# The written-out order of all five queues, shifted by small steps, in an attention and two-MLP kernel on one core

## The chip, the core and the metric

The kernel runs on one NeuronCore of a Trainium2 chip. The core has five engines with a queue each, and each executes its queue in order: TensorE (PE, matmuls, with the weight loads PEld beside it), VectorE (DVE), ScalarE (ACT), GpSimd (POOL) and SyncE (SP), which here issues the DMAs. The metric is the device time of one execution in microseconds, the median of several runs.

## What is computed

The input of 4 x 768 tokens goes through three parts: a gated delta-rule attention (8 heads of 48), an MLP whose token mixing is the real part of a two-dimensional Fourier transform, and an MLP whose token mixing is by two matrices.

```python
for t in range(S):                                   # attention, per batch and head
    y[t] = q[t] @ state
    state = state + b[t] * outer(kn[t], v[t] - kn[t] @ state)
x = y                                                # 4 x 768 x 384
u = x + real(fft(fft(x, axis=1), axis=2))            # first MLP
ch = relu(layernorm(u) @ w_ch1) @ w_ch2              # 384 -> 1536 -> 384
x = u + ch
theta = x @ w_theta                                  # second MLP
yr, yi = w_tok_r @ (x * cos(theta)), w_tok_i @ (x * sin(theta))
u = x + yr + yi
return u + relu(u @ w_ch)
```

## The kernel before

The attention is done by chunks of 64 tokens. `gram` multiplies keys and queries of a chunk (tiles `sm`, PE L351) and ACT evacuates them into `KQ` (L384); POOL moves a part of them within `KQ` (L386). `solve` inverts a triangular block on DVE: a transpose of `KQ` into `T` (L397), then thirty pairs of steps, `tmp` (L434) and `T` (L437), and a scaling (L438). Chunk pairs are numbered 0 to 23, and four of them make one solve, so that there are six solves, 0 to 5. `solved` transposes the result twice, into `TN` (L446) and `TT` (L448). `chunks` then makes for each chunk `pa` from `TN`, `A` (ACT L518), `pt` from `TT`, parts of `YU` by copies (L485) and by ACT (L531), and `pw`, which ACT evacuates into `YU` (L537). `scan` carries the state from chunk to chunk: `pu` (evacuated into `X`, L555 and L556), `ps` (into `X`, L566 and L567) and `py` (into `y`, L581 and L583). After the early phase `sm`, `pa`, `pt` and `pw` take turns in one PSUM bank (pool `psw`, `NMW` = 1).

While this runs, the weights of the first MLP, which are given as 64-bit floats, are converted chunk by chunk (`Split.steps`): DMA L239, ACT L242, four or five DVE steps (L243 to L249) and three PE matmuls into a tile whose name ends in `s` (L251 to L253). A chunk is named by its weight, its row block and its column, for instance `w1_2_768`.

When the first batch is scanned, `fourier_inputs` adds and subtracts six tiles `y` on DVE (L610), with two scalings on ACT (`y4` L626, `y1` L631), and folds them (L610). `fourier_1` multiplies the folds by cosines and sines (`pg`, PE L671). Then come `ffn_up` (`ph` L204 to L206, ACT `hh` L802, DVE `hl` L803) and `ffn_down` (`pc` L812 to L815, DVE `u` L818, store `x2scr` L819), twelve blocks of tokens, with the later scans in between.

The token mixer loads `xt` from `x2scr` (SP L1056), transposes it (`tt`, PE L1059), computes theta (`pth`), reduces it to a remainder `r` (DVE L1073 to L1075), takes sine and cosine on ACT (L1076 to L1078), multiplies by `xt` (DVE L1082) and splits the product in two (ACT L1085, POOL L1086, tiles named `w1h` and `w1l` in the trace because they lie in the weights' memory). `ty` multiplies these by the token matrices, `tc` by `w_ch`.

The order in every queue is written out. The table `ORDER` holds one string per engine. Each entry counts how far to jump in the order in which the program was written and how many instructions to take from there (`+8` after a jump of `32` reads `32+8`). `arrange` walks the strings and ties each instruction to the next one in its queue, without a semaphore:

```python
for a, b in zip(queue, queue[1:]):
    tc.add_manual_dep(b, a.name, edge, reason="order")
```

## Time and profile before

| | |
|---|---|
| median of 3 runs | 953.66 us (952.69 to 954.89) |
| the profiled execution | 952.9 us |
| its span in the trace | 951.1 us |
| PE busy | 877.6 us (92%) |
| DVE busy | 647.8 us (68%) |
| ACT busy | 431.3 us (45%) |
| POOL busy | 304.7 us (32%) |
| granted PE clock, mean | 0.930 |

The span is the time between the first and the last instruction of the profiled execution; the rest of its time lies around it. A busy share is over the whole span. The clock is given as a share of 2.4 GHz: 0.5 is the lower of the two levels, 1.2 GHz, and a value between the two is a mean over a stretch that had both.

### The profile page before, as it was taken

How to read it: one execution, taken by the hardware profiler on the slowest of the kernel's cores; microseconds unless marked ns; L12 is line 12 of the kernel's file. 1: busy time of each engine (PE TensorE's matmuls, PEld its weight loads, DVE VectorE, ACT ScalarE, POOL GpSimd, SP SyncE). 2: the span in 40 equal slices, each digit the busy share in tenths (PEclk: the TensorE clock that was granted, in tenths of full speed). 3: DMA queues.
4: the chain of work that ended last, by engine and by line, in shares of the span. 5: the costliest groups of instructions: out<-in, count | busy, mean ns of one | idle time of the engine just before them, and what ended most of it. 6: DMA issues, size and time to landing. Idle time of an engine off the chain costs nothing.

```text
span 951.1 us, 23435 instructions
## 1 busy us (share of the span) xinstructions
PE 877.6 (92%) x9408; PEld 795.2 (84%) x9408; DVE 647.8 (68%) x1494; ACT 431.3 (45%) x1068; POOL 304.7 (32%) x422
## 2 busy tenths in 40 slices
PE   3688878799999999999999999999998999999998
PEld 3566657678787988888889879998997999999997
DVE  7997889778798962988322588788778844625411
ACT  4357885356453335445324333322574634525300
POOL 3101422231331015314110554555144541534411
PEclk7558975599999999999999999999998999999999
DMA  7413733232421114212021232333023111111001
GB/s 207 149 57 103 222 106 97 86 84 87 128 75 58 35 36 126 68 36 77 27 67 36 84 100 68 100 100 117 17 68 119 49 58 35 50 42 37 22 13 47
DMA packets 42205, 73.58 MB, mean 77 GB/s; under 512 B 6001, under 2 KB 26225, under 8 KB 42097
## 3 DMA queue, kind: packets, MB, share of 16 engines
q1 hardware_dynamic: 41328, 69.72, 24.4%
q0 software_dynamic: 768, 2.36, 0.8%
q8 instruction: 74, 1.21, 0.6%
q14 instruction: 35, 0.28, 0.1%
HBM read 57.91 MB, written 14.16 MB: 76 GB/s over the span
## 4 chain that ended last, share of the span: by engine, by line
PE 71%; DVE 14%; DMA 5%; ACT 5%; issue 3%; SPq 1%; POOL 0%; POOLq 0%; DVEq 0%; ACTq 0%
PE ty L204 5%; PE ty L206 5%; PE ty L205 5%; PE ph L204 5%; PE pc L812 5%; PE pc L815 5%; PE ph L206 4%; PE ph L205 4%; PE pc L813 4%; PE sm L351 3%; PE pw L351 2%; PE py L351 2%; DVE tmp L434 2%; PE pg L671 2%; DVE T L437 2%
## 5 line engine op out<-in xcount | busy, mean ns | idle before, releaser
L204 PE MATMUL ph<-uh,w1h 128*128 128x256 f32 x432 | 125.4, 290 | 3.5 <-DVE un L760 1.6
L206 PE MATMUL ph<-uh,w1l 128*128 128x256 f32 x432 | 121.9, 282 | 0.0
L205 PE MATMUL ph<-ul,w1h 128*128 128x256 f32 x432 | 121.8, 282 | 0.0
L802 ACT ACTIVATE hh<-ph 128x256 fp32r<-128x256 f32 x144 | 55.0, 383 | 139.9 <-PE ph L206 67.4
L803 DVE SCALAR_TENSOR_TENSOR hl<-ph,hh 128x256 fp32r<-128x256 f32 x144 | 60.0, 420 | 77.5 <-ACT hh L802 49.0
L812 PE MATMUL pc<-w2h,hh 128*128 128x384 f32 x288 | 102.4, 356 | 1.2 <-DVE u L818 1.1
L815 PE MATMUL pc<-w2h,hl 128*128 128x384 f32 x288 | 94.6, 356 | 2.9 <-DVE hl L803 2.8
L813 PE MATMUL pc<-w2l,hh 128*128 128x384 f32 x288 | 96.9, 336 | 0.0
L351 PE MATMUL sm<-kt 48*64 48x128 f32 (+1 forms) x896 | 67.7, 312 | 27.4 <-DMA kt<-in_kq_dram 20.9
L204 PEld LDWEIGHTS ph<-uh,w1h 128*128 128x128 f32 x432 | 81.8, 189 | 7.7 <-DVE hl L803 2.8
L497 POOL TENSOR_SCALAR_AFFINE_SELECT YQ<-KQ 64x512 f32<-64x512 f32 x48 | 33.5, 699 | 168.0 <-PE py L351 148.3
L351 PEld LDWEIGHTS sm<-kt 48*64 48x64 f32 x896 | 56.2, 173 | 35.1 <-issue 13.8
L205 PEld LDWEIGHTS ph<-ul,w1h 128*128 128x128 f32 x432 | 81.9, 190 | 0.3
L206 PEld LDWEIGHTS ph<-uh,w1l 128*128 128x128 f32 x432 | 82.0, 190 | 0.0
L434 DVE TENSOR_TENSOR tmp<-T 128x30 f32<-128x30 f32 (+9 forms) x180 | 67.4, 375 | 4.5
L437 DVE TENSOR_TENSOR T<-T,tmp 128x30 f32<-128x30 f32 (+9 forms) x180 | 65.8, 366 | 5.4
L812 PEld LDWEIGHTS pc<-w2h,hh 128*128 128x128 f32 x288 | 54.3, 188 | 6.7 <-issue 1.9
L815 PEld LDWEIGHTS pc<-w2h,hl 128*128 128x128 f32 x288 | 52.4, 188 | 7.2 <-DVE hl L803 4.6
L813 PEld LDWEIGHTS pc<-w2l,hh 128*128 128x128 f32 x288 | 54.3, 189 | 0.1
L1122 POOL TENSOR_TENSOR w2l<-xT,w2h 128x384 fp32r<-128x384 f32 x24 | 25.0, 1045 | 91.6 <-ACT w2h L1121 91.6
L510 POOL TENSOR_TENSOR X<-X,nT 64x384 f32<-64x384 f32 x48 | 41.1, 858 | 37.2 <-DMA X<-in_v_dram 27.5
L1121 ACT ACTIVATE w2h<-xT 128x384 fp32r<-128x384 f32 x24 | 12.5, 524 | 69.5 <-DVE xT L1120 37.3
(307 smaller groups left out, 2297.4 us busy)
## 6 DMA issues: line engine op xcount, KB each, us to landing
kt<-in_kq_dram SPq DMA_DIRECT2D x48, 224.0 KB, 2.7
w_0raw<-in_w_dram SPq DMA_DIRECT2D x15, 384.0 KB, 5.0
YQ<-in_qt_dram SPq DMA_DIRECT2D x48, 96.0 KB, 2.9
X<-in_v_dram SPq DMA_DIRECT2D x48, 96.0 KB, 2.8
...
```

What stands on the lines that cost most here:

```text
L204: nc.tensor.matmul(out, lh, rh, start=start, stop=False)
L205: nc.tensor.matmul(out, lh, rl, start=False, stop=False)
L206: nc.tensor.matmul(out, ll, rh, start=False, stop=stop)
L351: self.nc.tensor.matmul(o, l, r, start=True, stop=True, skip_group_check=True)
L434: nc.vector.tensor_tensor(pr, E[:, :, j + 1:, j:j + 1].to_broadcast([P, nb, n, j]), E[:, :, j, 0:j].unsqueeze(2).to_broadcast([P, nb, n, j ...
L437: nc.vector.tensor_tensor(E[:, :, j + 1:, 0:j], E[:, :, j + 1:, 0:j], pr, ALU.add)
L510: nc.gpsimd.tensor_tensor(x[TK[par], par], x[TK[par], par], nT[TK[par], n].unsqueeze(2).to_broadcast([C, 8, D]), ALU.mult)
L802: nc.scalar.activation(hh, ph, AF.Relu)
L803: self.up_end = nc.vector.scalar_tensor_tensor(hl, ph, 0.0, hh, ALU.max, ALU.subtract)
L812: nc.tensor.matmul(self.pc[i], hh[:, i * P:(i + 1) * P], wh, start=(f == 0), stop=False)
L813: nc.tensor.matmul(self.pc[i], hh[:, i * P:(i + 1) * P], wl, start=False, stop=False)
L815: nc.tensor.matmul(self.pc[i], hl[:, i * P:(i + 1) * P], wh, start=False, stop=(f == KF - 1))
```

## The change

Only the table `ORDER` is written anew, for all five queues. The instructions and their data are the same: 6530 on PE, 1070 on ACT, 1496 on DVE, 427 on POOL and 357 on SP. 4859 of those on PE stand in another place (by 29 places in the mean, 219 at most), 820 on ACT (4 and 30), 1221 on DVE (5 and 76), 158 on POOL and 219 on SP (each under 2 in the mean). The new table is two lines longer, so that a line after it has a number higher by two. Two lines of the diff, of some 240:

```diff
 ORDER = {
...
-    "PE": """32+32 -64+32 32+179 111+16 -127+16 56+6 -62+16 70+3 -73+16 162+16 -178+8 49+6 16+16 83+16 -186+16 6+8 8+8 -16+8
...
+    "SP": """4+2 -4+2 33 -37 -2 23 2 2 -25 29 -8 -23 8 17 -4 6 -22 17 -22 8 -9 -8 19 -20 12 16 -30+2 29 -30+2 4+4 24 -22+2
...
```

At the end of solve 0 DVE had `TT0`, four copies into `YU0`, `TN0`, four copies into `YU1` among steps of two conversions, and the transpose into `T1`. Now it has `TN0`, `TT0`, one copy, the transpose into `T1`, and the other seven copies.

At the end of solve 1, PE. `py6` and `ps7` are steps of the scan, `sm11` is the last of the four `gram` chunks that solve 2 needs, `pa4` is the first user of `TN1`, and the three rows of `w1_2_768s` are the sums of a converted chunk. Before:

```order
L351 MATMUL ps7_1612<-X1_84,Y31_86 48x48 x8
L351 MATMUL py6_1562<-X1_84,YQ1_82 64x48 x8
L351 MATMUL sm11_4_0_1462<-kt11_4_0_1460 64x128 x8
L351 MATMUL py6_1562<-X1_84,YQ1_82 64x48 x8
L351 MATMUL pa4_1478<-TN1_1421,KQ1_248 32x32 x16
L351 MATMUL pt4_1498<-TT1_1423,A4_1495 32x32 x16
L251 MATMUL w1_2_768s_1439<-w1_2_768ag_1432,ident_61 128x384
L252 MATMUL w1_2_768s_1439<-w1l_95,eyes_87 128x384
L253 MATMUL w1_2_768s_1439<-w1h_94,eyes_87 128x384
L351 MATMUL sm11_0_0_1448<-kt11_0_0_1446 64x128 x8
```

After:

```order
L353 MATMUL py6_1562<-X1_84,YQ1_82 64x48 x8
L353 MATMUL ps7_1612<-X1_84,Y31_86 48x48 x8
L253 MATMUL w1_2_768s_1439<-w1_2_768ag_1432,ident_61 128x384
L254 MATMUL w1_2_768s_1439<-w1l_95,eyes_87 128x384
L255 MATMUL w1_2_768s_1439<-w1h_94,eyes_87 128x384
L353 MATMUL sm11_4_0_1462<-kt11_4_0_1460 64x128 x8
L353 MATMUL sm11_0_0_1448<-kt11_0_0_1446 64x128 x8
L353 MATMUL pa4_1478<-TN1_1421,KQ1_248 32x32 x16
L353 MATMUL pt4_1498<-TT1_1423,A4_1495 32x32 x16
```

The sums of `w1_2_768` and `sm11_0` have gone from behind `pa4` and `pt4` to ahead of them. The same place on DVE, before:

```order
L434 TENSOR_TENSOR tmp1_1308<-T1_1285 128x30
L437 TENSOR_TENSOR T1_1285<-T1_1285,tmp1_1308 128x30
L438 TENSOR_TENSOR T1_1285<-T1_1285,g_1_1290 128x1024
L448 STREAM_TRANSPOSE TT1_1423<-T1_1285 128x32x32
L446 STREAM_TRANSPOSE TN1_1421<-T1_1285 128x32x32
L243 TENSOR_SCALAR w1_2_768ag_1432<-w1_2_768raw_1431 128x384
L244 TENSOR_SCALAR w1_2_768ag_1432<-w1_2_768ag_1432 128x384
L245 SCALAR_TENSOR_TENSOR w1_2_768ag_1432<-w1_2_768ag_1432 128x384
L246 TENSOR_SCALAR w1_2_768ag_1432<-w1_2_768ag_1432 128x384
L249 SCALAR_TENSOR_TENSOR w1l_95<-w1_2_768raw_1431,w1_2_768ag_1432 128x384
L243 TENSOR_SCALAR w2_6_0ag_1572<-w2_6_0raw_1571 128x384
```

After:

```order
L247 SCALAR_TENSOR_TENSOR w1_2_768ag_1432<-w1_2_768ag_1432 128x384
L248 TENSOR_SCALAR w1_2_768ag_1432<-w1_2_768ag_1432 128x384
L251 SCALAR_TENSOR_TENSOR w1l_95<-w1_2_768raw_1431,w1_2_768ag_1432 128x384
L436 TENSOR_TENSOR tmp1_1308<-T1_1285 128x30
L439 TENSOR_TENSOR T1_1285<-T1_1285,tmp1_1308 128x30
L440 TENSOR_TENSOR T1_1285<-T1_1285,g_1_1290 128x1024
L450 STREAM_TRANSPOSE TT1_1423<-T1_1285 128x32x32
L448 STREAM_TRANSPOSE TN1_1421<-T1_1285 128x32x32
L245 TENSOR_SCALAR w2_6_0ag_1572<-w2_6_0raw_1571 128x384
L246 TENSOR_SCALAR w2_6_0ag_1572<-w2_6_0ag_1572 128x384
L247 SCALAR_TENSOR_TENSOR w2_6_0ag_1572<-w2_6_0ag_1572 128x384
L399 STREAM_TRANSPOSE T2_2090<-KQ2_1140 128x1024
```

The five steps that convert `w1_2_768` stand ahead of the last pair of solve 1 and of `TN1`, and the transpose of solve 2 (`T2`) has come up to three steps behind `TN1`; before it stood behind all of the next chunk's conversion and more.

At the end of the first batch's scan, ACT. `pu`, `ps` and `sm` are evacuated into `X` and `KQ3`, `y0_4` and `y0_1` are the tiles `y4` and `y1` of the Fourier inputs, and `e0` is one of their edge columns. Before:

```order
L556 ACTIVATE X1_84<-pu14_2315 64x192
L566 ACTIVATE X1_84<-ps14_2326 48x192
L567 ACTIVATE X1_84<-ps14_2326 48x192
L384 ACTIVATE KQ3_2352<-sm15_0_0_2459 128x512
L555 ACTIVATE X1_84<-pu15_2381 64x192
L556 ACTIVATE X1_84<-pu15_2381 64x192
L566 ACTIVATE X0_83<-ps15_2392 48x192
L626 ACTIVATE y0_4_1719<-y0_4_1719 128x385
L567 ACTIVATE X0_83<-ps15_2392 48x192
L384 ACTIVATE KQ3_2352<-sm15_4_0_2473 128x512
L656 ACTIVATE e0_0_1905<-t0_0_1868 128x1
L631 ACTIVATE y0_1_1001<-y0_1_1001 128x385
```

After:

```order
L539 ACTIVATE YU1_79<-pw7_2256 48x512 x2
L628 ACTIVATE y0_4_1719<-y0_4_1719 128x385
L557 ACTIVATE X1_84<-pu14_2315 64x192
L558 ACTIVATE X1_84<-pu14_2315 64x192
L658 ACTIVATE e0_0_1905<-t0_0_1868 128x1
L633 ACTIVATE y0_1_1001<-y0_1_1001 128x385
L386 ACTIVATE KQ3_2352<-sm13_0_0_2355 128x512
L651 ACTIVATE t1_0_1869<-y0_1_1001 128x1
L568 ACTIVATE X1_84<-ps14_2326 48x192
L569 ACTIVATE X1_84<-ps14_2326 48x192
L386 ACTIVATE KQ3_2352<-sm13_4_0_2369 128x512
L648 ACTIVATE y0_5_1862<-y0_2_1415 128x1
```

The scaling of `y4` goes from behind the first half of `ps15` to ahead of `pu14`, the scaling of `y1` from behind `sm15_4` to ahead of `sm13_0`.

At the hand-over to the token mixer, DVE. `r0_5` and `n0_5` are the last of the six remainders of the first batch, `wch_2_0` is a chunk of `w_ch`, `hl3_2_10` and `hl3_2_11` belong to the last feed-forward block, and `u3_2` is its output. Before:

```order
L1073 SCALAR_TENSOR_TENSOR r0_5_9444<-n0_5_9443,pth0_5_9433 128x384
L803 SCALAR_TENSOR_TENSOR hl3_2_10_9335<-ph3_2_10_9324,hh3_2_10_9334 128x256
L246 TENSOR_SCALAR wch_2_0raw_9401<-wch_2_0a_9402 128x384
L257 SCALAR_TENSOR_TENSOR wch_2_0raw_9401<-wch_2_0raw_9401 128x384
L262 TENSOR_TENSOR wch_2_0a_9402<-wch_2_0a_9402,w2h_96 128x384
L803 SCALAR_TENSOR_TENSOR hl3_2_11_9355<-ph3_2_11_9344,hh3_2_11_9354 128x256
L1074 SCALAR_TENSOR_TENSOR r0_5_9444<-n0_5_9443,r0_5_9444 128x384
L1075 TENSOR_SCALAR r0_5_9444<-r0_5_9444 128x384
L818 TENSOR_TENSOR u3_2_8615<-u3_2_8615,pc3_2_0_8969 128x384
L818 TENSOR_TENSOR u3_2_8615<-u3_2_8615,pc3_2_1_8970 128x384
L1082 TENSOR_TENSOR r0_5_9444<-r0_5_9444,xt0_5_9422 128x384
L1082 TENSOR_TENSOR n0_5_9443<-n0_5_9443,xt0_5_9422 128x384
```

After:

```order
L247 SCALAR_TENSOR_TENSOR wch_2_0a_9402<-wch_2_0a_9402,wch_2_0raw_9401 128x384
L248 TENSOR_SCALAR wch_2_0raw_9401<-wch_2_0a_9402 128x384
L1075 SCALAR_TENSOR_TENSOR r0_5_9444<-n0_5_9443,pth0_5_9433 128x384
L1076 SCALAR_TENSOR_TENSOR r0_5_9444<-n0_5_9443,r0_5_9444 128x384
L1077 TENSOR_SCALAR r0_5_9444<-r0_5_9444 128x384
L259 SCALAR_TENSOR_TENSOR wch_2_0raw_9401<-wch_2_0raw_9401 128x384
L264 TENSOR_TENSOR wch_2_0a_9402<-wch_2_0a_9402,w2h_96 128x384
L805 SCALAR_TENSOR_TENSOR hl3_2_11_9355<-ph3_2_11_9344,hh3_2_11_9354 128x256
L1084 TENSOR_TENSOR n0_5_9443<-n0_5_9443,xt0_5_9422 128x384
L820 TENSOR_TENSOR u3_2_8615<-u3_2_8615,pc3_2_0_8969 128x384
L820 TENSOR_TENSOR u3_2_8615<-u3_2_8615,pc3_2_1_8970 128x384
L1084 TENSOR_TENSOR r0_5_9444<-r0_5_9444,xt0_5_9422 128x384
```

The three steps of the remainder stand together, and `n0_5` is multiplied ahead of `u3_2`, `r0_5` behind it. On ACT the copy of `n0_5` now comes ahead of that of `r0_5`. On PE the first 36 matmuls of `ty0_0_0` stand together; before, `tt1_0` stood behind the first 18. `tt1_0` is still followed by other `ty` groups and transposes in turn.

## Rows read from the trace of the kernel before

**Rows 1.** Part 1 of the page: busy time of each engine

```profile
PE 877.6 (92%) x9408; PEld 795.2 (84%) x9408; DVE 647.8 (68%) x1494; ACT 431.3 (45%) x1068; POOL 304.7 (32%) x422
```

**Rows 2.** Windows: us; busy PE, PEld, DVE, ACT, POOL; clock; DMA share; GB/s

```profile
143.00:193.00 50.00, 41.38 (x613) 36.52 (x612) 41.21 (x100) 22.93 (x63) 13.49 (x22) 0.53 0.30 87
200.00:720.00 520.00, 504.86 (x5810) 451.59 (x5809) 371.81 (x906) 229.37 (x601) 173.70 (x241) 1.00 0.25 74
724.70:729.20 4.50, 4.50 (x15) 4.50 (x16) 3.25 (x6) 1.28 (x3) 2.48 (x2) 0.50 0.58 163
750.00:951.10 201.10, 196.54 (x1142) 195.08 (x1140) 83.31 (x146) 69.39 (x144) 67.83 (x72) 1.00 0.12 37
```

**Rows 3.** Waits of PE: releaser, us in total, times, longest

```profile
PE ps L351 <- ACT X L556: 1.7, 2, 0.8
...
PE sm L351 <- ACT YU L537: 1.2, 2, 0.7
```

**Rows 4.** Timeline: start, us, engine, operation, [idle before]; end of solve 0

```profile
52.38 1.96 DVE L448 STREAM_TRANSPOSE TT<-T 128x1024 f32<-128x1024 f32 x1
...
55.48 1.93 DVE L446 STREAM_TRANSPOSE TN<-T 128x1024 f32<-128x1024 f32 x1
...
57.55 1.07 PE L351 MATMUL pa<-TN,KQ 32*32 32x32 f32 x32 [3.05 <-DVE TN L446]
...
61.00 1.80 PE L351 MATMUL pw<-YU,Y 64*48 64x64 f32 x23 [0.46 <-ACT YU L531]
```

**Rows 5.** Timeline, DVE's two longest idle times in solve 1

```profile
79.60 0.36 DVE L244 TENSOR_SCALAR w_384ag<-w_384ag 128x384 f32<-128x384 f32 x1 [3.11 <-ACT w_384ag L242]
...
91.44 0.36 DVE L243 TENSOR_SCALAR w_384ag<-w_384raw 128x384 uint32<-128x384 uint32 x1 [1.94 <-PE w_384s L253]
```

**Rows 6.** Timeline, DVE and PE, end of solve 1

```profile
124.60 0.95 DVE L243 TENSOR_SCALAR w_768ag<-w_768raw 128x384 uint32<-128x384 uint32 x1
...
126.84 0.56 DVE L249 SCALAR_TENSOR_TENSOR w1l<-w_768raw,w_768ag 128x384 fp32r<-128x384 uint32 x1
...
133.66 1.99 DVE L397 STREAM_TRANSPOSE T<-KQ 128x1024 f32<-128x1024 f32 x1 [0.64 <-POOL KQ L386]
...
124.80 1.06 PE L351 MATMUL pa<-TN,KQ 32*32 32x32 f32 x32 [4.05 <-DVE TN L446]
...
128.11 1.65 PE L251 MATMUL w_768s<-w_768ag,ident 128*128 128x384 f32 x2
...
130.32 1.88 PE L351 MATMUL sm<-kt 48*64 48x128 f32 x16
```

**Rows 7.** Timeline, ACT, DVE and PE, the Fourier inputs

```profile
179.53 0.51 ACT L626 ACTIVATE y<-y 128x385 f32<-128x385 f32 x1
...
181.76 0.52 ACT L631 ACTIVATE y<-y 128x385 f32<-128x385 f32 x1
...
182.31 0.42 DVE L610 TENSOR_TENSOR t<-y 128x192 f32<-128x192 f32 x1 [6.22 <-ACT y L631]
...
185.07 0.80 PE L671 MATMUL pg<-cs,y 128*128 128x128 f32 x2 [3.94 <-DVE y L610]
```

**Rows 8.** Timeline, PE and SP, the hand-over to the token mixer

```profile
716.89 0.33 PE L204 MATMUL ty<-wtrh,w1h 128*128 128x384 f32 x1
...
719.33 0.34 PE L206 MATMUL ty<-wtrh,w1l 128*128 128x384 f32 x1
...
720.61 0.44 PE L204 MATMUL ty<-wtrh,w1h 128*128 128x384 f32 x1 [0.94 <-ACT w1h L1085]
722.30 0.55 PE L206 MATMUL ty<-wtrh,w1l 128*128 128x384 f32 x1 [1.08 <-POOL w1l L1086]
724.70 0.87 PE L1059 MATMUL tt<-ident,xt 128*128 128x128 f32 x3 [1.86 <-DVE wti_0a L244]
...
718.67 0.56 SPq L819 DMA_DIRECT2D x2scr<-u  x1
722.04 1.75 SPq L1056 DMA_DIRECT2D xt<-x2scr  x4
```

More of the change, by code (lines that the diff above doesn't have):

```diff
@@ L80 @@
 ORDER = {
-    "PE": """32+32 -64+32 32+179 111+16 -127+16 56+6 -62+16 70+3 -73+16 162+16 -178+8 49+6 16+16 83+16 -186+16 6+8 8+8 -16+8
[46 rows of a table removed]
- 63+18 -81+18 27+18 18+18 -81+9 72+63""",
-    "Activation": """0 6+6 -12+2 1+3 -4 9+2 24 -25+2 23 -24+2 46 -25 24 -48+3 46 -47+4 52 -10 -44+13 3 38 -3 -37+2 1 -2 1+2 40+4
[22 rows of a table removed]
- -21 1 -2 1+2 16 -13+3 1 -2 9+3 2+2 6 -20 19 -8+2 1 -8 5 5 -5 4 1 -24 21 1 -16 7 -17 23+7""",
-    "DVE": """6 -7 7 6 -15+2 6 -7 6 -4 -4 11 -12 6 -2 1+2 2+7 4 -5+4 1+2 61+5 -66+2 74+3 -77+4 73+2 -75+4 71+2 -73+2 71+3
[25 rows of a table removed]
- -10 14 -6+5 1+3 -18 17+2 -19 18+6 3 -4+3 1+5""",
-    "Pool": """59 -59 15 4 17 8 2 4+2 -55+2 10 -2 -14+2 -4 9+2 1+2 -3 -7+4 29 -21 -2 1+2 1+2 3 -2 1+2 1 -2 -7+2 6+4 4+2 -6+2
[7 rows of a table removed]
- -2 3 5 -3 4 -3 -7 8 -6 -4 5 2+7""",
-    "SP": """4+2 -4+2 19 -24 26 -27 22 -19 21 7+2 -4 -28 27 -5 6 -9 -2 -14+2 4 -15 6 -2 -6 29 -30 30 -31+2 33 -34 4+4 3+2 5+2
[6 rows of a table removed]
- -4 4 6+3 -11 4+2 4 -5 4 3+2 -16+3 13 3 -10+3 7+2 3+3 -12 14 -15+2 3+3 7+2 -6+3 3+9""",
+    "PE": """32+32 -64+32 32+163 127+16 -143+32 56+6 -62+16 70+3 -73+24 154+16 -162+8 33+3 -52+8 44+3 -33+8 41+16 83+16
[46 rows of a table added]
+ 63+36 -63+9 72+18 -90+18 36+18 18+36 27+18 18+18 -81+18 27+18 -45+9 54+81""",
+    "Activation": """0 6+6 -12+2 1+3 -4 9+6 20+2 24 -25 -23+4 43 -44+2 43 -44+2 51 -52+2 40 -41+9 41 -42 3 38 -39+8 39 -2 1+2 -42+2
[23 rows of a table added]
+ -5 4 1 -24 21 1 -16 7 -17 23+7""",
+    "DVE": """9 2 -12+2 -3 14 -10 -4+2 5 2 -3 -7 1+2 5 1+12 1 62 -65 1+2 61+4 10 -76+3 73+2 -75+7 68+2 -70+11 59 -60 59 -60 59
[26 rows of a table added]
+ 14 -6+5 1+3 -18 17+2 -19 18+6 3 -4+3 1+5""",
+    "Pool": """59 -59 56 -42 4 17 8 2 4 -54 -3 13 -2 -13 1 -6 9 2+2 -3 -2 -6+4 29 -22+4 1+4 1 -2 1+2 1 -2 1+4 4+2 4+2 -12+2
[7 rows of a table added]
+ 9+6""",
+    "SP": """4+2 -4+2 33 -37 -2 23 2 2 -25 29 -8 -23 8 17 -4 6 -22 17 -22 8 -9 -8 19 -20 12 16 -30+2 29 -30+2 4+4 24 -22+2
[6 rows of a table added]
+ -11 4+3 3+2 3+2 -16+3 13 3 -10+3 7+2 3+3 3 -16+3 3+3 7 -5+2 3 -4 3+9""",
 }
```

214 rows, old and new, of the table ORDER are left out of this document.

## The prediction

> **What bounds the kernel now.** I read the shares first. TensorE (PE) is busy 92% of a span of 951.1 us [rows 1], so the end is set by PE's own work, by the time it stands idle and by the clock at which it runs. The table by stretch divides this up [rows 2]. From 200 to 720 us PE is busy 504.86 of 520 us at clock 1.00, and from 750 on 196.54 of 201.1, the rest being the last evacuations. Only 15.1 us of idle time are to be had in the long middle, in many small pieces. From 143 to 193 us PE is busy 41.38 of 50 us at a granted clock of 0.53, which means almost all of it at 1.2 GHz. There a wait is not the only loss: work at half speed costs twice its time.
>
> A change of order alone can remove no work. It can remove waits and it can move the clock. So I looked for the long waits, and for the engine that each ended on. Three places stand out. At 57.55 and 124.80 us PE waits 3.05 and 4.05 us for a transpose on VectorE (DVE), `TN` [rows 4, 6]. At 185.07 us it waits 3.94 us for the folds of the Fourier inputs, because DVE had itself stood 6.22 us waiting for a scaling on ScalarE (ACT) [rows 7]. Around 720 to 725 us it waits 0.94, 1.08 and 1.86 us where the feed-forward part hands over to the token mixer [rows 8].
>
> **Part 1, the two solves (50 to 133 us).** After solve 0 DVE ran the transpose `TT` at 52.38, four copies, and only then `TN` at 55.48. Now `TN` is first, so `pa0` may start up to 55.48 - 52.38 = 3.1 us earlier. What follows it, `pw0` at 61.00, also needs `TT`, the copies into `YU` and an ACT step; these come about 1.5 us earlier (estimate: half of 3.1, since `TT` is later by the 1.93 us of `TN`). This only gives PE earlier filling work. The pace up to 125 us is DVE's chain, since PE waits for it at both ends.
>
> In that chain DVE stands idle 3.11 us at 79.60 for an ACT step of a weight conversion and 1.94 us at 91.44 for the buffers of the one before [rows 5]. The changed order groups conversions otherwise, and both waits may go or return elsewhere. I take back 3 of the 5.05. Against that, the five DVE steps of the conversion `w1_2_768` are put ahead of the end of solve 1. They ran from 124.60 to 127.40, the first of them in 0.95 us [rows 6] where one of its shape takes 0.36 [rows 5]; without that excess they cost 2.2 us. `TN1` is thus from 2.2 us later to 3 us earlier, say 1 earlier.
>
> For PE the same move is a gain. The sums of `w1_2_768` (130.32 - 128.11 = 2.21 us) and `sm11_0` (1.88 us) stood behind the wait for `TN1` and now stand ahead of `pa4`: 4.09 us of work goes into a hole of 4.05 us. If `TN1` is 2.2 us late the net is 1.9 us, if it is on time or early 4.1 to 5.4 (with the 1.5 us of earlier filling work as the limit). A new wait can eat part of it: the transpose of solve 2 goes from 133.66 to just behind `TN1`, and it needs the copies of `sm11_0` on Pool, for which it waited 0.64 us even there [rows 6]. If it waits 2 us, the conversion of `w2_6_0` and the first fold queue behind it on DVE, and PE's sums for that chunk wait for them. Together **3.5 us, ends 0 and 5.4**.
>
> **Part 2, the Fourier inputs (143 to 193 us).** On ACT the scaling of `y4` (L626) ran at 179.53 and that of `y1` (L631) at 181.76. Ahead of them in the queue stood evacuations of `ps15` and `sm15_4`, which PE delivered late at half clock. DVE's last instruction before its idle time ended at 182.31 - 6.22 = 176.1, so `y4` had been ready for about 3.4 us. Now `y4` stands behind `pu13`, `ps13` and `pw7`, and `y1` behind `pu14`, five evacuation groups earlier. By the earlier delivery of these the scaling of `y1` can end about 4.5 us sooner. The folds behind it need 185.07 - 182.31 = 2.76 us before PE can go on, so PE would find them at about 180.5, while its queue ended at 181.13 (185.07 - 3.94). The wait of 3.94 us goes nearly whole. The scan's steps are also interleaved otherwise with `sm13` and `sm15`, which can remove the two waits of 0.85 us for `X` and one of 0.6 [rows 3]. But `pw7` now stands straight ahead of `pu14`, which reads what ACT evacuates from it; that wait is new, and I price it at 0.6 to 1.7 us from the same row and the 0.85. **4 us, ends 1 and 5**. The lower end is the case in which `pu14` is late on PE and carries the scaling with it.
>
> DVE gets up to 6 us of slack here, in front of the end of solve 2. That is not counted: PE is the later of the two from 193 on.
>
> **Part 3, the hand-over (713 to 730 us).** DVE computed the last remainder `r0_5` in three steps with three conversions and two `hl` between them. Now the three stand in a row, and `n0_5`, which PE needs first, is scaled and copied ahead of `r0_5` on DVE and ACT. The waits of 0.94 and 1.08 us [rows 8] should go, though `pth0_5` stands nearer to the end of the feed-forward part than before, and I leave up to 0.5 us. PE then has 36 matmuls instead of 18 ahead of `tt1_0`. One takes (719.33 - 716.89) / 14 = 0.174 us, so the block is 6.3 us. `tt1_0` names a DVE step as its releaser, but that step has nothing to do with its operand: the load of `xt` was issued at 722.04, 3.37 us behind the store at 718.67, and 2.66 us later the transpose ran. Store to transpose is 6.03 us. The store itself waits for `u`, which now stands behind `n0_5` on DVE and so 0.2 to 0.7 us later than before (718.67 - 716.89 = 1.78 after the first `ty`). The transpose is ready 8.0 to 8.5 us after the first `ty`, and PE reaches it after 6.3 to 6.8: a wait of 1.2 to 2.2 us stays. Of 3.88 us go 1.2 to 2.7. Behind the wait came 4.5 us at clock 0.50 with 15 matmuls, where 15 x 0.174 = 2.6 would do: 1.9 us that may or may not go too. **2.5 us, ends 0 and 5**.
>
> **Part 4, the rest.** Between 200 and 720 us hundreds of instructions move, up to 219 places on PE. With 15.1 us of idle time in all, and waits that I can't follow one by one, I count 0, with ends of 3 us lost and 6 gained. The last 200 us have almost the same order: 0.
>
> **Sum.** 3.5 + 4 + 2.5 + 0 = 10 us off the profiled execution of 952.9 us (the span and 1.8 us around it, which stay): 942.9. The median of the runs shown, 953.66, lies 0.8 above that execution, so the forecast for a median is **943.7 us**. All low ends together would be 2 us slower (about 955.7), all high ends 21.4 us faster (932.3).
>
> **Rivals.** *No change.* The gains of parts 1 and 2 are PE's, but DVE's chain of solves could set the pace up to 193 us. For it speaks that PE waits for it at 57, 124 and 185. Against it speaks that PE is busy 41.38 of 50 us just behind. If only the hand-over's smallest part stays, and the middle loses that: 951.8 to 955.6, say 953.5.
>
> *Slower: the one PSUM bank.* After the early phase `sm`, `pa`, `pt` and `pw` share one bank of PSUM. Each user waits until ACT has emptied the one before, and ACT works in order, with `hh` and the others in its queue. The row of `sm` behind `YU` shows 0.6 us a time [rows 3]. There are 67 such hand-overs in the order between 200 and 700 us. Where two users stand close together in the new order, PE waits. Up to 17 new waits of 0.6 us eat the gain of 10. With 30 of them it is 953.7 - 10 + 18 = 961.7. Against it: the pairs stand no closer on the whole. Those with two or three short groups between them go from 33 to 30, and only `pt8` and `pw8` now touch.
>
> *Faster by the clock.* From 143 to 193 us 41.38 us of work ran at about half clock. If fewer waits bring the full clock at 170 instead of 193, then 23 x 41.38 / 50 x 0.5 = 9.5 us more are won: 934.2. For it: from 200 us on, where PE is hardly ever idle, the clock is 1.00 [rows 2]. Against it: PE was 83% busy from 143 to 193 us and the clock stayed down. Besides, the order takes the long sums of `w1_0_1152` from just ahead of that stretch into it, so the fall may as well come earlier. The Trainium skill ("TensorE: Matmul & The Clock Gate", section "HAM oscillation — how this bites in real kernels") describes a second way to a low clock besides long waits: PE idles for moments between matmul groups as PSUM buffers are cycled, and the clock swings. The trace agrees in part: small groups through one bank, 83% busy, clock 0.53; by the page's rule fewer gaps would lift it.
>
> **Chances.** The forecast, anywhere from 4 to 18 us faster: 0.64. Faster by the clock: 0.08. No change: 0.12. Slower: 0.16, nearly all of it the bank. A measurement of this kernel tells about 0.2% (1.9 us) from no change. Faster is thus 0.72, the same 0.12, slower 0.16. The range of 932 to 957 us takes in the ends of the sum, most of the clock's case and the mild half of the bank's.
>
> **What would show it.** Part 1: `pa4` without a wait of over 1 us, and DVE's two idle times at 80 and 91 gone; wrong if DVE waits for `KQ` ahead of `T2`. Part 2: L631 ends before 178.5 and `pg` waits under 1 us. Part 3: `ty` runs 36 matmuls with under 0.5 us of waits, and `tt1_0` still waits 1 to 2 us for its load. Part 4: PE idle between 200 and 720 us within 9 to 18 us; over 22 the bank has decided. The forecast is wrong if the clock's mean over 60 to 200 us moves by over 0.05 either way, since that is worth 7 us or so.

## The result, and the profile after

The changed kernel takes **957.11 us** (median of 11 runs, 954.89 to 960.65), the kernel before 952.69 in the same session (11 runs, 946.84 to 956.72). The ratio is **1.0064, interval 1.0040 to 1.0089**: slower by 0.6%, some 6 us, where 10 us less were forecast. (The quotient of the two medians is 1.0046, inside that interval. Here and below I go by the ratio that comes with the interval.) The profiled execution of after has a span of 954.8 us, against 951.1.

All ratios below are to the kernel before, run beside it on the same chip; 0.1% is 0.95 us. A time or a wait of a trace is that of one run of its kernel; for h135, h62, hc, hin, hmid and l_notDVE it was the slowest of all its runs, so the ratios carry the argument. Line numbers of after are 2 higher than those of before.

Part 1 of the page of after, held against [rows 1], tells little: PE is busy 876.4 us where it was 877.6, DVE 643.0 where it was 647.8. It is the same work in the same sum. The stretches tell more. Windows of after; columns as in [rows 2]:

```profile
60.00:143.00 83.00, 67.17 (x1031) 50.71 (x1027) 62.64 (x160) 57.95 (x143) 21.63 (x36) 0.79 0.43 128
143.00:193.00 50.00, 40.34 (x691) 34.50 (x690) 45.96 (x109) 26.38 (x72) 15.23 (x29) 0.73 0.30 88
193.00:230.00 37.00, 32.07 (x434) 27.31 (x433) 23.07 (x58) 16.74 (x43) 10.04 (x20) 0.77 0.29 85
200.00:720.00 520.00, 503.58 (x5799) 451.87 (x5800) 363.36 (x894) 225.72 (x593) 168.54 (x238) 0.98 0.24 72
720.00:750.00 30.00, 27.49 (x163) 26.66 (x163) 24.96 (x50) 14.93 (x31) 11.88 (x12) 1.00 0.37 109
```

Three of them for before, which the rows ahead of the prediction don't hold:

```profile
60.00:143.00 83.00, 68.93 (x1147) 53.02 (x1142) 69.32 (x159) 62.61 (x154) 22.04 (x38) 0.81 0.43 126
193.00:230.00 37.00, 34.88 (x595) 29.43 (x595) 29.13 (x84) 21.35 (x56) 10.40 (x23) 0.99 0.29 86
720.00:750.00 30.00, 26.46 (x141) 25.71 (x142) 24.95 (x46) 17.45 (x38) 15.24 (x15) 0.89 0.35 105
```

Read them in pairs. In 60 to 143 us DVE does 6.7 us less in after (62.64 against 69.32): it stands idle more, at the place where its idle time was to shrink. In 143 to 193 us the clock rose from 0.53 to 0.73, at nearly the same busy time: the Fourier inputs gained. (Of this rise a part is scatter: in the four other kept traces with the old order up to 191 us, those of h230, h690, hin and i_copies below, the clock there was 0.59 to 0.62.) In 193 to 230 us the clock fell from 0.99 to 0.77 and PE is idle 4.9 us instead of 2.1. At the hand-over, 720 to 750 us, PE is busier and the clock is whole.

To add this up I use a *lag*, my own working: each group of matmuls gets one price, its short duration in the two traces, and the lag is how much later than in the trace of before PE has done work of the same total price. For after it is +5.2 us at 135, +0.6 at 190, **+9.6 at 230**, +7.5 at 690 and +3.7 at the end. Another choice of the price gives 10.4 at 230 and the same elsewhere, so a lag is good to about 1 us. So there are two losses (up to 135, and 190 to 230) and three gains.

**The first loss** is DVE's. Its idle times of over 1 us before TN1 in after, where before had three (the two of [rows 5] and 1.64 us for a load at 106.57):

```profile
85.92 0.36 DVE L245 TENSOR_SCALAR w_384ag<-w_384raw 128x384 uint32<-128x384 uint32 x1 [1.85 <-DMA w_384raw<-in_w_dram]
...
92.46 0.37 DVE L246 TENSOR_SCALAR w_0ag<-w_0ag 128x384 f32<-128x384 f32 x1 [1.40 <-ACT w_0ag L244]
...
99.16 0.36 DVE L245 TENSOR_SCALAR w_0ag<-w_0raw 128x384 uint32<-128x384 uint32 x1 [4.76 <-DMA w_0raw<-in_w_dram]
101.11 0.36 DVE L246 TENSOR_SCALAR w_0ag<-w_0ag 128x384 f32<-128x384 f32 x1 [1.59 <-ACT w_0ag L244]
...
115.80 0.36 DVE L245 TENSOR_SCALAR w_768ag<-w_768raw 128x384 uint32<-128x384 uint32 x1 [2.42 <-DMA w_768raw<-in_w_dram]
```

The 6.7 us of before are gone, and 12.0 us of others have come. They are all of one kind: a weight conversion whose chunk isn't loaded, or not yet scaled by ACT, stands in DVE's queue, and the scan steps of solve 1 stand behind it. TN1 starts at 126.69, against 122.80 before. One trace of each would be little to go by, but the experiments below left more. In the five with the new order up to here, idle times of over 1 us add up to 11.5 to 17.8 us and TN1 starts at 124.37 to 133.88; in the seven with the old order they add up to 4.4 to 6.7 us and TN1 starts at 120.68 to 122.80. So the new order is later here in every trace, and far less steady.

The end of solve 1, DVE, PE and ACT of after; [rows 6] answers:

```profile
126.69 2.02 DVE L448 STREAM_TRANSPOSE TN<-T 128x1024 f32<-128x1024 f32 x1
...
125.46 0.91 PE L253 MATMUL w_768s<-w_768ag,ident 128*128 128x384 f32 x2
...
126.65 1.96 PE L353 MATMUL sm<-kt 48*64 48x128 f32 x32
128.76 0.69 PE L353 MATMUL pa<-TN,KQ 32*32 32x32 f32 x32
133.45 0.77 PE L353 MATMUL pt<-TT,A 32*32 32x32 f32 x8 [4.00 <-ACT A L520]
...
127.95 1.31 ACT L386 ACTIVATE KQ<-sm 128x512 f32<-128x512 f32 x2
129.16 0.55 ACT L244 ACTIVATE w_0ag<-w_0raw 128x384 f32<-128x384 f32 x1
129.73 3.27 ACT L485 ACTIVATE YU<-TT 32x256 f32<-32x256 f32 x8
133.02 0.78 ACT L520 ACTIVATE A<-pa 32x256 f32<-32x256 f32 x2
```

The fill works as it was meant: the sums and `sm` stand ahead of `pa4`, and `pa4` doesn't wait. But the next step, `pt4`, waits 4.00 us for `A`. The same eight copies into `YU` stood ahead of `A` on ACT in before as well; there they ran from 122.99 us, while PE stood waiting for `TN1`, and `pt4` waited only 0.86 us:

```profile
122.99 3.28 ACT L483 ACTIVATE YU<-TT 32x256 f32<-32x256 f32 x8 [0.87 <-DVE TT L448]
...
126.72 1.45 PE L351 MATMUL pt<-TT,A 32*32 32x32 f32 x32 [0.86 <-ACT A L518]
```

Now ACT first evacuates the `sm` that was brought forward and scales a chunk, so that the copies start at 129.73, 2.9 us after `TT1` is there (126.83), and `A` comes behind them. The hole of 4.05 us has moved by one step.

**The second loss**, PE and DVE of after from 193 us:

```profile
193.80 2.21 PE L749 MATMUL pm<-cs,G 128*128 128x385 f32 x6
...
202.21 1.95 PE L353 MATMUL pw<-YU,Y 64*48 64x64 f32 x32 [4.02 <-DVE YU L487]
...
196.05 0.55 DVE L755 TENSOR_TENSOR u<-u,pm 128x384 f32<-128x384 f32 x1 [3.17 <-PE pm L749]
...
197.28 0.95 DVE L487 COPY YU<-TT 32x256 f32<-32x256 f32 x2
...
199.54 2.73 DVE L487 COPY YU<-TT 32x256 f32<-32x256 f32 x5
```

After solve 2 DVE has twelve copies into `YU` to make, four into each of three tiles: `YU2`, which `pw8` reads, `YU0`, which `pw9` reads, and `YU1`, which `pw10` reads. In before eleven ran first, and all four of `pw8` were among the first seven. Now the four of `pw9` run (191.70 to 192.88 us), then DVE waits 3.17 us for `pm` from PE, and the other eight, with all four of `pw8`, stand behind that wait. PE in its turn waits 4.02 us for the last copy into `YU2`. So it waits for an engine that had waited for it, and the copies that ran in time were not the ones that came due. The row of `pw8` in before, and the copies:

```profile
198.88 1.17 PE L351 MATMUL pw<-YU,Y 64*48 64x64 f32 x32 [0.26 <-ACT YU L531]
...
193.44 3.28 DVE L485 COPY YU<-TT 32x256 f32<-32x256 f32 x11
```

Behind the wait came half clock: windows of after, 200 to 220 us, where before shows 1.00 throughout:

```profile
200.00:205.00 5.00, 2.29 (x34) 2.11 (x35) 4.34 (x13) 0.98 (x3) 1.43 (x2) 0.56 0.26 81
205.00:210.00 5.00, 5.00 (x65) 4.25 (x65) 2.50 (x6) 3.16 (x8) 0.49 (x2) 0.50 0.11 14
210.00:215.00 5.00, 5.00 (x56) 4.16 (x54) 2.07 (x6) 2.72 (x7) 0.83 (x3) 0.50 0.48 159
215.00:220.00 5.00, 5.00 (x75) 4.31 (x73) 2.11 (x6) 2.37 (x6) 1.00 (x3) 0.74 0.47 130
```

Of the 9.0 us of lag gained here, 2.8 are more idle time (4.9 against 2.1); the other 6.2 I put down to PE being busy at half speed. That split is worked out, not shown by a run.

### The profile page after: what moved, and what is told of

The parts are those of the page before. It is cut to its first block, busy times and chain, and to the rows that moved or that the text cites. A ratio compares the mean times of both kernels' runs of the same rounds, so it can differ in the third digit from the quotient of the medians.

```text
span 954.8 us, 23383 instructions
## 1 busy us (share of the span) xinstructions
PE 876.4 (92%) x9408; PEld 794.9 (83%) x9408; DVE 643.0 (67%) x1494; ACT 430.3 (45%) x1068; POOL 306.5 (32%) x422
## 4 chain that ended last, share of the span: by engine, by line
PE 66%; DVE 6%; DMA 4%; ACT 2%; issue 2%; POOL 1%; SPq 0%; POOLq 0%; ACTq 0%; DVEq 0%
PE ph L206 5%; PE ty L206 5%; PE ty L207 5%; PE ty L208 5%; PE pc L814 5%; PE pc L817 5%; PE ph L207 4%; PE ph L208 4%; PE pc L815 4%; PE sm L353 3%; PE pg L673 2%; PE pm L749 2%; PE pu L353 2%; PE py L353 2%; PE tc L207 1%
## 5 line engine op out<-in xcount | busy, mean ns | idle before, releaser
L206 PE MATMUL ph<-uh,w1h 128*128 128x256 f32 x432 | 127.6, 295 | 3.6 <-DVE un L762 2.0
L353 PE MATMUL sm<-kt 48*64 48x128 f32 (+1 forms) x896 | 70.2, 322 | 29.0 <-DMA kt<-in_kq_dram 22.7
L353 PEld LDWEIGHTS sm<-kt 48*64 48x64 f32 x896 | 59.1, 180 | 35.7 <-issue 11.3
L388 POOL COPY KQ<-KQ 32x128 f32<-32x128 f32 x64 | 22.3, 349 | 98.3 <-ACT KQ L386 87.9
```

The source lines that it names most:

```text
L206: nc.tensor.matmul(out, lh, rh, start=start, stop=False)
L353: self.nc.tensor.matmul(o, l, r, start=True, stop=True, skip_group_check=True)
```

## The experiments

Most of these kernels join the two orders: each queue takes first what the one order starts before a certain time of its trace, then the rest in the other order. The arithmetic is the same in all. "Before 135 us" thus names a set of instructions.

**s1_sp: the loads earlier.** The changed kernel, three weight loads moved ahead in SP's queue:

```
-Y31, X1, YQ1, ysc, w2_4raw ... kt9, w2_5raw ... YQ0, Y30, X0, w1_1_768raw
+w2_4raw, Y31, X1, YQ1, ysc ... w2_5raw, kt9 ... w1_1_768raw, YQ0, Y30, X0
```

> The changed kernel with three loads of raw weights moved up in SP's queue: w2_4 and w2_5 ahead of the loads Y31, X1, YQ1 and kt9, and w1_1_768 ahead of YQ0, Y30, X0. Theory (SP's queue): in the changed kernel the load of Y31 blocked the queue until 90.7 us and six loads behind it held w2_4 back until 95.3, so that DVE stood 4.8 and 2.4 us; with the loads moved DVE's idle time between 85 and 118 us falls from 13 to under 6, the transpose TN1 ends 4 to 6 us earlier (near 123 instead of 128.7), and the time is 3 to 5 us under the changed kernel's: ratio to the kernel before 1.001 to 1.004. Rival (ACT's queue): ACT's part of the same conversions stands behind evacuations of sm9 that come no earlier, DVE waits for ACT instead of the DMA, TN1 moves under 1.5 us, ratio 1.005 to 1.008.

Measured: 957.52 us, ratio 1.0076 [1.0043, 1.0109]; TN1 at 128.49 in its profiled execution. The ratio is the rival's. The wait for the load of `w2_4` went, and this came in its place (DVE's timeline of this kernel, and PE's):

```profile
102.28 0.36 DVE L241 TENSOR_SCALAR w_0ag<-w_0ag 128x384 f32<-128x384 f32 x1 [9.45 <-ACT w_0ag L239]
...
93.67 2.10 PE L348 MATMUL pw<-YU,Y 64*48 64x64 f32 x32 [3.50 <-DMA Y<-in_kn_dram]
```

This load was not the cause: the same conversion then waits for ACT's scaling, and that stands behind evacuations of `pw` and `sm`, which PE delivers only then. Loads as such are not ruled out by it, since `pw` in turn waits 3.50 us for that of `Y31`, one of those that the weights had been moved ahead of.

**s2_copies: the copies back in front.** The changed kernel, eight `YU` copies of DVE ahead of the first `u`:

```
 DVE: YU0 copies x4
-u0_0<-pm, YU1, u0_0<-pm, YU2 x2, bn, mv, YU1 x2, YU2 x2, YU1
+YU2 x4, YU1 x4, u0_0<-pm x2, bn, mv
```

> The changed kernel with the eight copies into YU2 and YU1 that follow the solve's transpose TT2 put back ahead of DVE's first residual u (which waits for pm). Theory (DVE's queue at 192 us): the wait of 4.0 us of pw8 at 202 goes and the clock does not fall to half from 201 to 216; the time is 5 to 9 us under the changed kernel's: ratio 0.997 to 1.001. Rival (the clock falls anyway, or the 4 us come back at the next wait for un): under 2 us, ratio 1.004 to 1.007.

Measured: 955.98 us, 1.0024 [0.9990, 1.0057]. PE's timeline of this kernel:

```profile
197.80 1.10 PE L348 MATMUL pw<-YU,Y 64*48 64x64 f32 x32 [0.86 <-ACT YU L528]
200.89 1.12 PE L786 MATMUL pt<-ident,un 128*128 128x128 f32 x4 [2.00 <-DVE un L776]
```

The ratio lies between the two ranges that were expected. The long wait is gone, and perhaps 0.4% with it (1.0064 to 1.0024, intervals that overlap). But in the profiled execution the clock was 0.50 from 200 to 220 us all the same, beside the wait of 2.00 us for `un`: in the new order the transposes of `un` stand directly behind `pw8`. PE's lag grew there by as much as in after.

**h190_after_before and h690_before_after: two cuts.**

```
-h190: old order throughout
+h190: new order until 191.5 us, old order for the rest
-h690: old order throughout
+h690: old order until 690 us, new order for the rest
```

> Everything that the changed kernel had started by 191.5 us in its order, all the rest in the order of the kernel before. Theory (the loss of solve 1 is made good by the Fourier inputs at 193 us, the net loss lies behind): within 2 us of the kernel before, ratio 0.998 to 1.002. Rival (the early stretch is where the loss stays): ratio 1.003 to 1.007.

> The order of the kernel before for everything that it had started by 690 us, the changed order for the rest: the hand-over to the token mixer alone. Theory: 3 to 5 us faster than the kernel before, ratio 0.995 to 0.997; ty runs 36 matmuls without a wait over 0.5 us and tt1_0 waits about 1 us. Rival (the gain at the hand-over was only the making good of what the changed kernel lost at 650 to 690): within 1.5 us, ratio 0.9985 to 1.0015.

Measured: h190 954.33 us, 1.0017 [0.9984, 1.0050]; h690 949.48 us, 0.9967 [0.9936, 0.9999]. Both ratios are as expected. The hand-over alone gives 0.33%, 3.1 us. Up to 191 us the new order is no gain.

**hin_191_230, hc_135_191, hmid and h230_before_after: four slices.**

```
-old order throughout
+hin:  old until 191.5 us, new until 230, old for the rest
+hc:   old until 135 us, new until 191.5, old for the rest
+hmid: new until 191.5 us, old until 230, new for the rest
+h230: old until 230 us, new for the rest
```

> The order of the kernel before, with the changed order between 191.5 and 230 us alone. Theory (as for hmid, the fault put in alone): the clock falls to half at about 200 us for 10 to 20 us, PE is 5 to 9 us behind at 225 us, and 2 to 6 us of it stay at the end: ratio 1.002 to 1.006. Rival (the fall needs what the changed order does earlier): clock 1.00 from 200 to 225 us, ratio 0.998 to 1.002.

> The order of the kernel before up to 135 us and from about 192 us on, with the changed order in between: part 2 of the prediction alone. Theory (part 2 works, but its lead is given back near 300 us, where PE waits for un and DVE has been over 90% busy since 230 us): pg starts 3 to 6 us earlier than in the kernel before, PE leads by 3 to 5 us at 200 us and by under 1.5 us at 330 us, ratio 0.998 to 1.001. Rival (the lead lasts to the end): ratio 0.995 to 0.997.

> The changed order up to 191.5 us and again from 230 us on, with the order of the kernel before for what that had started by 230 us in between. Theory (the net loss is made between 192 and 222 us, where DVE's copies for pw8 stand behind a wait for pm and the transposes of un stand straight behind pw8; the two waits are followed by some 15 us at half clock): granted clock 1.00 from 200 to 225 us and the time 4 to 9 us under the changed kernel's, ratio to the kernel before 0.995 to 1.001. Rival (the lead is given back wherever it is made, since DVE sets the pace until 345 us): under 3 us, ratio 1.003 to 1.007.

> The order of the kernel before up to 230 us, the changed order for all the rest. Theory (between 230 and 690 us the new order neither wins nor loses; only the hand-over wins): as the hand-over alone, ratio 0.995 to 0.998. Rival (close users of the one PSUM bank, the prediction's slower case): waits of PE for YU, KQ and A between 230 and 690 us grow by over 4 us in all, ratio 1.000 to 1.004.

Measured: hin 962.28 us, **1.0096** [1.0060, 1.0133]; hc 948.92 us, 0.9968 [0.9938, 0.9998]; hmid 948.04 us, 0.9956 [0.9928, 0.9983]; h230 946.03 us, **0.9913** [0.9878, 0.9947]. The slice of 191 to 230 us, in which 54 instructions of DVE and 290 of PE stand in another place, costs nearly 1%, more than was expected. hmid is the changed kernel with this slice taken back: from 1.0064 to 0.9956. The Fourier inputs gain 0.32%; the theory that their lead is given back later was wrong, the rival was right. From 230 us on the new order gains 0.87%, which neither expectation of h230 had; 0.33 of it is the hand-over. So 0.54% come from the long middle, for which the prediction counted 0 and its slower rival a loss. With two intervals of 0.3% each way this is hardly clear of nothing.

**i_copies: the copies alone.** The kernel before, with DVE's queue changed in one place:

```
-YU1, YU2 x3, YU1, YU0, YU2, YU1, YU0 x3, u0_0<-pm x2, bn, YU1, bn, mv
+YU0 x4, u0_0<-pm x2, bn, YU1, bn, mv, YU1, YU2 x3, YU1, YU2, YU1
```

> The kernel before with one difference: seven of the eleven YU copies that VectorE does ahead of the first u0_0 stand behind it, as in the new order; TensorE's order is the old one. Theory (the copies queued behind the wait for pm are enough): pw8 waits some 4 us, TensorE falls to half clock for 10 to 20 us near 200 us, ratio 1.003 to 1.010. Rival (it takes the transposes pt0 directly behind pw8 as well): the clock stays at 1.00 in 200 to 220 and the ratio is 0.999 to 1.003.

Measured: 960.00 us, **1.0066** [1.0030, 1.0102]. PE's timeline, and the stretch behind:

```profile
200.42 0.41 PE L346 MATMUL pw<-YU,Y 64*48 64x64 f32 x2 [3.74 <-DVE YU L480]
201.25 1.94 PE L346 MATMUL pw<-YU,Y 64*48 64x64 f32 x30 [0.42 <-DVE YU L480]
```

```profile
200.00:205.00 5.00, 3.19 (x42) 2.70 (x44) 1.92 (x7) 1.39 (x3) 0.98 (x2) 0.50 0.12 36
205.00:210.00 5.00, 5.00 (x76) 4.35 (x74) 1.42 (x6) 1.92 (x6) 0.57 (x2) 0.66 0.17 51
```

Seven copies behind one wait, the four of `pw8` among them, and nothing else, cost 0.66% where the whole slice costs 0.96. This is shown: the copies alone are enough for a loss. What the rest is due to (the transposes of `un`, or something else in the slice) was not separated. Nor was the likely cure tried, the four copies into `YU2` ahead of those into `YU0`.

**h135_after_before, h62_after_before: the early stretch.**

```
-old order throughout
+h135: new order until 135 us, old order for the rest
+h62:  new order until 62 us, old order for the rest
```

> The new order for what it starts before 135 us, the old order for all the rest. Theory (the regrouped conversions of the first solves cost time that stays lost): TN1 starts 2 to 5 us later than in the kernel before (122.8), ratio 1.003 to 1.008. Rival (a late TN1 is made good by slack in the Fourier inputs, and the early stretch costs nothing at the end): ratio 0.998 to 1.002 although TN1 is as late.

> The new order until 62 us, so that only the earlier TN0 and pa0 are kept, and the old order from there. Theory (the first 62 us are harmless, the loss of the early stretch comes from the order of the conversions in 62 to 135): TN1 starts 0 to 3 us earlier than 122.8, ratio 0.997 to 1.001. Rival (the early TN0 itself brings the loss, by putting the conversions off): TN1 2 us or more later, ratio 1.002 to 1.006.

Measured: h135 958.93 us, **1.0087** [1.0057, 1.0117], TN1 at 133.88 in its profiled execution; h62 952.86 us, 0.9996 [0.9965, 1.0027], TN1 at 119.91. The earlier `TN` of solve 0 is harmless, and no gain of it can be measured at the end. The loss lies behind it, in 62 to 135 us.

**j_62_118, j_118_138: which of the two places.**

```
-old order throughout
+j_62_118:  old until 62 us, new until 118, old for the rest
+j_118_138: old until 118 us, new until 138, old for the rest
```

> The old order until 62 us, the new one for what it starts before 118, the old one for the rest. Theory (the regrouped conversions of 62 to 118 bring the whole loss of the early stretch): TN1 2 to 6 us later than 122.8, ratio 1.005 to 1.010. Rival (the loss is that of the end of solve 1, where solve 2's transpose now stands right behind TN1 and five conversion steps stand ahead of it): ratio 0.998 to 1.002.

> The kernel before with the new order only for what it starts in 118 to 138 us: the five conversion steps ahead of TN1, the sums of w1_2_768 and sm11_0 ahead of pa4, solve 2's transpose right behind TN1. The prediction's sizing of that place (4.09 us of work into a hole of 4.05, less up to 2.2 us by which TN1 is later): pa4 without a wait, ratio 0.995 to 0.999. Rival (what PE gains there it waits for again at the next transpose, since VectorE sets the pace): pa4 without a wait, ratio 0.999 to 1.003.

Measured: j_62_118 963.22 us, **1.0124** [1.0069, 1.0179]; j_118_138 953.95 us, 1.0012 [0.9980, 1.0043]. The stretch of 62 to 118 us, with its regrouped conversions, brings the loss; the fill ahead of `pa4`, which the prediction took for the gain of this place, brings nothing that can be measured. PE's timeline of j_118_138 shows why, as after did:

```profile
121.92 1.65 PE L246 MATMUL w_768s<-w_768ag,ident 128*128 128x384 f32 x2 [2.65 <-DVE w_768ag L240]
...
128.27 1.06 PE L346 MATMUL pa<-TN,KQ 32*32 32x32 f32 x32 [0.45 <-DVE TN L441]
132.66 1.46 PE L346 MATMUL pt<-TT,A 32*32 32x32 f32 x32 [3.33 <-ACT A L513]
```

Waits of 4.05 us for `TN` and 0.86 for `A` became 2.65 for the conversion, 0.45 for `TN` and 3.33 for `A`: 4.91 us became 6.43.

**k_scan: the scan ahead of the conversion.** The changed kernel, DVE's queue at 94 us:

```
-w2_4 conversion (4 steps), T 238, T 234, T 228, w2_4 (last step), T 220
+T 238, T 234, T 228, T 220, w2_4 conversion (5 steps)
```

> The changed kernel with eight VectorE instructions moved: the scan steps of solve 1 with 238, 234, 228 and 220 elements stand ahead of the conversion of w2_4_0 instead of behind its waits. Theory (the scan waits in the queue behind a conversion that waits for a load and for ScalarE): VectorE's idle time of 4.8 and 1.6 us at 94 to 101 us shrinks to about 3, TN1 is 2 to 4 us earlier than 126.7, ratio to the kernel before 1.002 to 1.005. Rival (the conversions are as much on the path as the scan, since TensorE's sums of them come due): TN1 within 1 us of 126.7, ratio 1.005 to 1.008.

Measured: 960.00 us, 1.0071 [1.0035, 1.0108]; TN1 at 131.36 in its profiled execution. The ratio is the rival's, though its interval reaches into the theory's range. DVE's waits in 60 to 135 us became others (3.9 us for a load, 3.7 for ACT, 2.6 for PE), and their sum was no smaller. The time of TN1 decides nothing here, since in the unchanged new order it lay anywhere from 124.37 to 133.88. That the scan isn't alone on the path is thus likely, not shown.

**l_DVE, l_notDVE: one queue or the others.**

```
-old order throughout
+l_DVE:    order of 62 to 118 us new in DVE's queue alone
+l_notDVE: order of 62 to 118 us new in all queues but DVE's
```

> The kernel before with the new order of 62 to 118 us in VectorE's queue alone (86 instructions stand elsewhere), all other queues as before. Theory (the loss lies in the other queues: ScalarE's scalings of the weight chunks stand behind the copies of KQ and pw, which wait for TensorE, and SP loads the chunks later; VectorE only waits for these): ratio 0.998 to 1.003. Rival (VectorE's own regrouping, scan steps behind conversions, brings the loss): ratio 1.006 to 1.012, TN1 3 us or more later than 122.8.

> The kernel before with the new order of 62 to 118 us in the queues of TensorE, ScalarE, Pool and SP, and VectorE's queue as before. Theory (these queues bring the loss): ratio 1.008 to 1.014, VectorE's long idle times at 94 to 101 us (4.8 and 1.6 us) are there although its own order is the old one. Rival (VectorE's own queue brings it): ratio 0.998 to 1.003.

Measured: l_DVE 957.88 us, 1.0063 [1.0037, 1.0089]; l_notDVE 960.92 us, 1.0088 [1.0067, 1.0110]. Neither expectation holds as a whole: each half costs by itself, and the two together (1.0124) about as much as their sum (1.0151), within the intervals. A window of each, 92 to 122 us, first of before, then of l_DVE, then of l_notDVE:

```profile
92.00:122.00 30.00, 25.28 (x426) 19.63 (x422) 26.23 (x60) 24.43 (x62) 11.64 (x23) 1.00 0.67 192
```

```profile
92.00:122.00 30.00, 25.46 (x354) 19.68 (x350) 23.92 (x58) 20.88 (x52) 10.02 (x20) 0.89 0.58 165
```

```profile
92.00:122.00 30.00, 22.09 (x326) 16.91 (x324) 17.54 (x41) 17.76 (x43) 9.47 (x18) 0.87 0.53 158
```

In before DVE is busy 26.2 of 30 us and the clock is whole. With the other queues changed DVE falls to 17.5, by waits for loads and for ACT (4.36 us for the load of `w2_4` among them), though its own order is the old one. With DVE's alone changed, PE waits 2.29 us for a remainder that DVE makes later. The place of the early loss is thus shown, 62 to 118 us in all queues. Its kind (conversions and their loads grouped so that DVE, ACT and PE wait for one another in turn) is read from the waits, and no single instruction is shown to cause it. Neither of the two cures tried (loads, scan) gave it back.

**best1, best2: the gaining slices together.**

```
-old order throughout
+best1: old until 135 us, new until 191.5, old until 230, new for the rest
+best2: new until 62 us, old until 118, new until 191.5, old until 230, new for the rest
```

> The old order for what starts before 135 us, the new one from there to 191.5, the old one again to 230, the new one for the rest. Theory (the losses of the new order lie before 135 and in 191 to 230, and its gains of 0.3% in 135 to 191, of 0.5% in 230 to 690 and of 0.33% in the hand-over add up): ratio to the kernel before 0.986 to 0.992, and pw8 waits under 2 us. Rival (the gain of 135 to 191 is lost again at 200 to 220, since TensorE falls to half clock there whatever the order): 0.990 to 0.996, with half clock in the windows 200 to 215.

> The new order until 62 us, the old one to 118, the new one to 191.5, the old one to 230, the new one for the rest. Theory (the end of solve 1 adds a gain to the ones of the kernel that measured 0.993): ratio 0.988 to 0.992. Rival (it adds nothing or takes some away): 0.992 to 0.997.

Measured: best1 944.63 us, **0.9930** [0.9896, 0.9965]; best2 943.79 us, **0.9896** [0.9843, 0.9948]. Both beat both kernels. Between the two the intervals don't decide, and `pt` waits 3.32 us in best2 as in j_118_138. best1 lies just outside its expected 0.986 to 0.992 and within the rival's range, though the rival's half clock in 200 to 215 us did not come (1.00). The sum of its slices, 0.988, is itself good to some 0.45% only, so that a shortfall isn't shown. Nor is either of the two shown to be better than h230, the single cut that measured 0.9913.

## Why the prediction was wrong

The slices price each part of the sum by itself (gains positive, us of 953, each uncertain by some 3):

| part | forecast | ends | measured | from |
|---|---|---|---|---|
| 1, the solves, to 135 us | 3.5 | 0 to 5.4 | -8.3 | h135 |
| 2, Fourier inputs | 4 | 1 to 5 | 3.0 | hc |
| 3, hand-over | 2.5 | 0 to 5 | 3.1 | h690 |
| 4, 191 to 230 us | in 0 | | -9.1 | hin |
| 4, 230 to 690 us | in 0 | -3 to 6 | 5.1 | h230 less h690 |

The measured column adds up to -6.2 us; the ratio of 1.0064 is -6.1. With some 3 us of uncertainty in each row, so close an agreement is partly luck. The slices that agree best in the traces are parts 2 and 3. In all nine kept traces with the new order from 135 to 191 us the lag falls there by 3 to 7 us, and in all nine with it at the hand-over it falls from 690 us on by 2.2 to 3.8; with the old order it changes by 1.3 at most in either. For 230 to 690 us the traces of the two orders overlap, so the 5.1 of the table is the weakest figure in it.

**Part 1 is the step that failed first.** "I take back 3 of the 5.05" assumed that the idle times of [rows 5] shrink in a new grouping. They went, and 12.0 us of the same kind came, since every conversion waits for a load, an ACT step and a buffer, each in a queue of its own whose place had moved too. The text had said that they "may go or return elsewhere", and then priced only the going. `TN1`, forecast from 2.2 us later to 3 earlier, came 3.9 later in after, and 1.6 to 11.1 later in the five traces named above. The test that was named, the two idle times at 80 and 91 gone, came true while the stretch lost 8 us: it tested two waits, not DVE's idle time as a whole. The sign named for being wrong, DVE waiting for `KQ` ahead of `T2`, came as well, with 0.88 us at 130.62. The other step, 4.09 us of work into a hole of 4.05, was right about `pa4` and wrong about what is late next: the evacuation of the `sm` brought forward holds up the eight `YU` copies that stand ahead of `A` on ACT. In j_118_138, with this step alone, 4.1 us less 2.2 at most were to be gained, and nothing that could be measured was. The lower end of part 1 should have lain well below zero.

**Part 2 was right in its mechanism.** The scaling of `y1` ran at 177.88, ending ahead of the 178.5 named, and the 3.94 us at `pg` went ([rows 7]; ACT and PE of after):

```profile
177.88 0.53 ACT L633 ACTIVATE y<-y 128x385 f32<-128x385 f32 x1 [1.09 <-DVE y L612]
```

```profile
186.48 0.79 PE L673 MATMUL pg<-cs,y 128*128 128x128 f32 x2
```

The time of `pg` is later than in before since after came 5 us late into the stretch. 3.0 us at the end against 4 is within the ends.

**Part 3 was right in size, and in detail but for one wait.** `ty` runs without waits, and `tt1_0` still waits, though 0.87 us and not 1.2 to 2.2 ([rows 8]; PE of after). A wait that the forecast had not came in front of them, for ACT's `hh` in the last feed-forward block:

```profile
724.99 0.44 PE L814 MATMUL pc<-w2h,hh 128*128 128x384 f32 x1 [1.64 <-ACT hh L804]
...
733.43 0.52 PE L1061 MATMUL tt<-ident,xt 128*128 128x128 f32 x3 [0.87 <-DVE wti_0raw L248]
```

Such a wait, of 1.64 to 1.96 us, stands in all nine traces with the new order here, and before has none. So the waits shrank by 1.4 us (3.88 to 2.51), within the 1.2 to 2.7 forecast only just, and the rest came with the half clock behind `tt1_0` (724.7 to 729.2), which in after is gone. The lag falls by 3.8 us there, the time by 3.1 in the ratio of the slice.

**Part 4 failed where it said 0.** The long middle was priced by PE's idle time, and the test named was 9 to 18 us of it between 200 and 720. After shows 520 - 503.58 = 16.4: within the test, and yet 9 us were lost at its front, since most of the loss was clock and not idle time (0.98 instead of 1.00 over 520 us), and part of the wait stood just outside. The order showed eight copies going behind `u`; I had not asked, for a wait of DVE on PE, what of PE's own operands stands behind it. The text even names the place, "only `pt8` and `pw8` now touch", but looked there for the PSUM bank and not for the copies. The ends of -3 to 6 were too narrow for hundreds of instructions that nobody had followed.

**The rivals.** The one bank of PSUM brought no loss that can be seen: from 230 to 690 us, with most of its hand-overs, the new order gains if anything. Why was not looked into. *Faster by the clock* came true in part: the clock over 143 to 193 us rose from 0.53 to 0.73, the lag fell by 4.6 us from 135 to 190, and behind 200 us the clock was lost again. The clock over 60 to 200 us, which was to tell by a change of 0.05, went from 0.72 to 0.78; but five kept traces with the old order up to 191 us have 0.72 to 0.78 there and four with the new one (after, s2, h190, hmid) 0.75 to 0.82, so that this test can't be read from one pair. The Trainium skill ("TensorE: Matmul & The Clock Gate", section "HAM oscillation — how this bites in real kernels") tells of waits for data after which each stretch starts at the low clock. The trace agrees in 200 to 217 us of after: a wait of 4.02 us, then 0.50. Waits of 2.00 us in s2_copies and 1.72 in h62 came with 0.50 behind them as well. (What the prediction drew from that page, the idling between groups as PSUM buffers are cycled, stands in its section "A second HAM failure mode: psum-queue depth-cycling"; no run here separates it from waits.) My forecast had asked where such waits would go, and not where the new order would make one.
